# A state-space scan in front of a GELU feed-forward block, one core: VectorE's steps on w_out, the transfers, and the sums of w_in in another order around the first group

## The chip, the cores and the metric

The kernel runs on one core of a Trainium2 chip. A core has five engines that run side by side, each with its own queue that is worked off in order: TensorE (PE, matrix products), VectorE (DVE), ScalarE (ACT), GpSimd (POOL) and SyncE (SP, which here issues nearly all DMA transfers). The metric is the time of one execution on the device in microseconds (us), lower is better; a kernel's time is the median of its runs.

## What is computed

The reference has two blocks. The first is a state-space recurrence (Mamba-2 style) over 4 batches, 8 heads and 768 positions, in chunks; the second is a feed-forward block with an approximate GELU on the 3072 tokens of 256 features that the first one leaves:

```python
# per batch and head; cum is the running sum of log a in a chunk
L = exp(cum_i - cum_j) * causal
y_intra = ((C @ B.T) * L) @ x
y_inter = (C @ state) * exp(cum)
state = exp(sum of log a) * state + sum_j B_j x_j exp(cum_last - cum_j)
# on tokens x 256
h = x @ w_in                      # 256 x 2048
g = h * sigmoid(1.702 * h)
out = g @ w_out                   # 2048 x 256
```

`w_in` and `w_out` come as 64-bit floats. The chip computes in 32 bits, so the kernel reads them as 32-bit words and makes the 32-bit floats itself.

## The kernel before, in words

**Groups and pairs.** The 3072 tokens are six groups of 512. A group is two *pairs* (`PG` = 2), a pair two chunks of 128 tokens. So group 0 holds pairs 0 and 1, group 1 pairs 2 and 3, and so on. While TensorE does the feed-forward products of one group, the other engines prepare the recurrence of the next.

**Group 0** does its feed-forward block plainly: `hidden(0, f)` for f from 0 to 15 (line 893; two products by a block of 128 columns of `w_in`, and SiLU on ScalarE), then `project_all` (line 989), which goes through f = 0 to 15 again with the rows of `w_out`. From group 1 on, each block goes by seven products in place of eight (`first`, `product`, lines 933 and 1030); that needs sums of blocks of the weights (`mix_in` for w_in, line 907, `mix_w` for w_out) and of the data (`mix_y`, `mix_g`).

**The weights** come in ten pieces (`PIECES`, line 154): pieces 0 to 5 are `w_in`, 6 to 9 `w_out`, four blocks each for the large ones. One piece takes these steps:

- `fetch(i)` (line 163): two DMAs on SP into one of four buffers;
- `fields(i)` (lines 192, 195): two VectorE steps that cut out exponent and mantissa;
- `clamp(i)` (lines 203, 204): two ScalarE steps on the exponent;
- `rounded(i)` (line 208): one VectorE step on the mantissa;
- `join(i)` (lines 222, 228): VectorE, two steps for each part; the second writes `w_in` or `w_out`. Only now can TensorE use the piece.

`narrow(i)` (line 235) is the VectorE part of one turn: `rounded(i)`, `join(i)`, and `fields(i + 1)`, in an order that hangs on i. `project_all` needs piece 6 at f = 0, piece 7 at f = 4, 8 at f = 8 and 9 at f = 12.

**The recurrence of pairs 2 and 3.** A pair needs its decay matrix L, made by a VectorE scan over the a values. For pair 2 the values are fanned out by TensorE (`fan_all`, line 424) into PSUM, and four scans read them there (`decay_heads`, line 457); `ends` (line 468) makes the values at chunk ends (tile Be); `since_fanned` (lines 548, 550) makes the decay since a chunk's start for the last chunks of batch 0, out of another PSUM bank. For pair 3 the values go by way of DRAM: `store_a` clips them on VectorE (line 358) and writes them to `scratch` (line 1232), `spread(3)` (line 261) reads them back to all partitions (tile a), and `decay(3)` (line 409) scans. `spread_rows(1)` (line 270) reads the a values of batch 1 (tile af); `clip_rows(1)` and `decay_rows(1)` (lines 487 to 500; VectorE, then POOL, then VectorE) turn them into the decay since the chunk's start. `turn(p)` transposes B and C of a pair on TensorE (line 604), copies them on ScalarE (line 597), and ends with `since_start` (line 674, tile CsT) on VectorE, which for pairs 2 and 3 reads the transposed C in its PSUM bank. `gain` (line 720, tile A) multiplies B by x for the states and takes the PSUM banks that the transposes of the two pairs used. Then come `score` (line 689), the additions of `keep_both` (line 789), `weigh` (line 700), and `finish` (lines 829 and 843), which leaves the input of group 1's feed-forward block.

**What sets the order.** Everything is written out by hand: `at(in_hidden[0], f, ...)` puts work behind `hidden(0, f)`, `at(in_project[0], f, ...)` ahead of the products of f in `project_all`. Entries of one place run in the order in which the `at` calls were made. A last step ties every engine's queue to the order of the program, so a waiting instruction holds all that stands behind it on its engine. PSUM gives the feed-forward products four banks in turn; the fanned rows, transposes, `gain` and `project_all`'s two sums take their banks from the same four.

Of the kernel before, what the change touches and what calls it, by code (L numbers as in the profile page):

```python
# [16 lines left out]
P = 128  # L17
# [18 lines left out]
def kernel(  # L36
# [48 lines left out]
    PG = CG // 2  # L85
# [52 lines left out]
    def load(p, parts=None):  # L138
        if parts is None:
            parts = "bcx" if p < 2 * PG else "bx"  # L140
            if p >= 2 * PG:
                load_blocks(p)
        for part in parts:
            dst, src, e = {"b": (rb, B, N), "c": (rc, C, N), "x": (rx, x, D)}[part]
            dst[p] = raw.tile([P, 2, NH, e], FP32, tag=part, name=f"{part}{p}",
                              bufs=2 if part == "c" else 3)
            for k in range(2):
                b, c = divmod(2 * p + k, NC)
                sl = slice(c * P, (c + 1) * P)
                nc.sync.dma_start(out=dst[p][:, k], in_=src[b, :, sl, :].rearrange("h s d -> s h d"))  # L150
# [12 lines left out]
    def fetch(i, held=False):  # L163
        name, f, n = PIECES[i]
        if n == 2 and f % 4:
            t = pieces.pop(i - 1)[:, 2 * n * DM:]
        else:
            t = pieces[i] = words(f"bits{i}")
            t = t[:, :2 * n * DM]
        if held:  # L170
            held.memset(t[:, :1], 0)
        if name == "in":
            src = moe_w_in[:, 2 * f * P:2 * (f + n) * P].rearrange("(k p) e -> p k e", p=P)
            dst, src = (v.rearrange(s, h=n, e=2 * P) for v, s in (
                (t, "p (h k e) -> k p h e"), (src, "p k (h e) -> k p h e")))
        else:
            src = moe_w_out[f * P:(f + n) * P, :].rearrange("(f p) (h e) -> h p f e", p=P, h=2)
            dst = t.rearrange("p (h f e) -> h p f e", h=2, f=n)
        for k in range(2):
            nc.sync.dma_start(out=dst[k], in_=src[k])  # L180
        t = t.rearrange("p (e w) -> p e w", w=2)
        bits[i] = t[:, :, 0], t[:, :, 1]
# [5 lines left out]
    def fields(i):  # L188
        hi, cols = bits[i][1], slice(0, PIECES[i][2] * DM)
        mantissa[i] = wide.tile([P, PN], U32, tag="m", name=f"m{i}")[:, cols]  # L190
        power[i] = wide.tile([P, PN], U32, tag="p2", name=f"p2{i}")[:, cols]
        nc.vector.tensor_scalar(out=power[i], in0=hi, scalar1=0x7FF00000, scalar2=None,
                                op0=ALU.bitwise_and)

        nc.vector.tensor_scalar(out=mantissa[i], in0=hi, scalar1=0x000FFFFF,
                                scalar2=0x00100000, op0=ALU.bitwise_and, op1=ALU.bitwise_or)
# [18 lines left out]
    def join(i, parts=1):  # L215

        name, f, n = PIECES[i]
        n //= parts
        low, m, p2 = bits.pop(i)[1], mantissa.pop(i), power.pop(i)
        for k in range(parts):  # L220
            cols, fs = slice(k * n * DM, (k + 1) * n * DM), slice(f + k * n, f + (k + 1) * n)
            nc.vector.scalar_tensor_tensor(out=p2[:, cols], in0=low[:, cols], scalar=0x80000000,
                                           in1=p2[:, cols], op0=ALU.bitwise_and, op1=ALU.bitwise_or)
            if name == "in":
                dst, h = w_in[:, fs].rearrange("p f k e -> p (f k e)").unsqueeze(1), 1
            else:
                dst, h = w_out[:, :, fs].rearrange("p c f e -> p c (f e)"), 2
            nc.vector.scalar_tensor_tensor(  # L228
                out=dst, in0=m[:, cols].bitcast(FP32).rearrange("p (h e) -> p h e", h=h),
                scalar=2.0 ** -20, in1=p2[:, cols].bitcast(FP32).rearrange("p (h e) -> p h e", h=h),  # L230
                op0=ALU.mult, op1=ALU.mult)
        for n in NEXT.get(i, ()):
            fetch(n)

    def narrow(i):
        rounded(i)
        if i in (2, 4, 5):
            join(i, 1 if i == 2 else 2)
        if i == 4:
            clip(az[:, CG:], 1)  # L240
        if i + 1 < len(PIECES):
            fields(i + 1)
        if i not in (2, 4, 5):
            join(i, 2 if i == 3 else 1)


# [3 lines left out]
    def spread(p, held=False):  # L250

        if p - 2 in ra:
            ra[p] = ra[p - 2]
        else:
            ra[p] = words(f"a{p}").bitcast(FP32)[:, :2 * NH * H].rearrange(
                "p (k e) -> p k e", k=2)
        if held:
            nc.vector.memset(ra[p][:, 0, :1], 0.0)
        b, c = divmod(2 * p, NC)
        for i, side in enumerate(SIDES):  # L260
            nc.sync.dma_start(
                out=ra[p][side],
                in_=scratch[c:c + 2, i, b * NH:(b + 1) * NH].rearrange("c h i -> c (h i)").unsqueeze(
                    0).to_broadcast([H, 2, NH * H]))
# [3 lines left out]
    def spread_rows(b):  # L268
        raf[b] = raw.tile([P, NC, P], FP32, tag="af", name=f"af{b}", bufs=1)
        nc.sync.dma_start(out=raf[b].rearrange("p c s -> p (c s)"),  # L270
                          in_=a[b].unsqueeze(1).to_broadcast([NH, N, S]))
# [84 lines left out]
    def clip(t, name):  # L356

        nc.vector.tensor_scalar(out=t, in0=t, scalar1=1e-6, scalar2=1.0,
                                op0=ALU.max, op1=ALU.min)
        if name:  # L360
            starts[name] = const.tile([P, t.shape[1], 2], FP32, name=f"starts{name}")
        first = t.rearrange(by_chunk, s=2)[:, :, :, 0]
        if name:
            nc.vector.tensor_copy(starts[name], first)
        nc.vector.memset(first, 0.0)
# [58 lines left out]
    def fan_all(p):  # L424

        ab = area(f"ab{p}")[:, :, :2 * Q * H]
        for r in range(R):
            fan(p, r, ab[:, r])
        fan_since()
        for r in range(R):  # L430
            decay_heads(p, r, ab[:, r])
        for k in range(2):
            ends(p, k)
# [99 lines left out]
    def fan_since():  # L533
        o = bank("rows4")
        t = fanned["rows"] = fan_rows(az, CG, NC, o)
        f = fanned["starts"] = o[:, 2 * P:2 * P + 2 * (NC - CG)]
        nc.tensor.matmul(out=f, lhsT=whose[:32, 0].rearrange("p h n -> p (h n)"),
                         rhs=starts[1][:32].rearrange("p c s -> p (c s)"), start=True, stop=True,
                         tile_position=(0, 0), skip_group_check=True)
# [678 lines left out]
    join(1)  # L1218
    fields(2)
    clamp(2)  # L1220
    load(PG)


    def at(places, i, *work):
        places.setdefault(i, []).extend(work)
# [5 lines left out]
        for i, side in enumerate(SIDES):  # L1231
            nc.sync.dma_start(out=scratch[:, i].rearrange("c r i -> r c i"), in_=az[:32, :, side])

    at(in_hidden[0], 5, lambda: fetch(7), lambda: fetch(8), lambda: load(PG + 1))
    at(in_hidden[0], 7, lambda: pick_a(PG))
    at(in_hidden[0], 9, lambda: fan_all(PG))
    at(in_hidden[0], 9, since_fanned, store_a)
    for i, k, c in ((2, 1, 1), (3, 2, 2), (4, 4, 7), (5, 8, 11), (6, 11, 14), (7, 14, 15)):
        at(in_hidden[0], k, lambda i=i: narrow(i))
        at(in_hidden[0], c, lambda i=i: clamp(i + 1))  # L1240
    at(in_hidden[0], 9, lambda: spread(PG + 1), lambda: spread_rows(1))
    n, p = 2 * PG, 3 * PG
    pairs = PG, PG + 1
    at(in_project[0], 0, lambda: turn(PG), lambda: rounded(8),
       lambda: fields(9), lambda: join(8))
    at(in_project[0], 1, lambda: clamp(9))
    at(in_project[0], 2, lambda: decay(PG + 1), lambda: clip_rows(1),
       lambda: decay_rows(1), lambda: turn(PG + 1))
    at(in_project[0], 5, lambda: narrow(9))
    at(in_project[0], 9, lambda: score(pairs), lambda: gain(pairs), lambda: keep_both(pairs, True),  # L1250
       lambda: weigh(PG), lambda: weigh(PG + 1))
    at(in_project[0], 15, lambda: finish(pairs))
    at(in_project[0], 13, lambda: mix_in(1), lambda: spread(n + 1, held=True),
       lambda: load(n + 1, "x"), lambda: mix_in(2), lambda: mix_in(3),
       lambda: turn_blocks(2), lambda: decay(n))
    at(in_project[0], 6, lambda: spread(n), lambda: load(n), lambda: load_blocks(n + 1),
       lambda: load(n + 1, "b"))

# [4 lines left out]
    at(after, "H0", lambda: decay(n + 1), lambda: mix_y(1), lambda: since_start(n),  # L1263
       lambda: since_start(n + 1), lambda: gain(later), lambda: keep_both(later, True), lambda: score(later),
       lambda: weigh(n), lambda: weigh(n + 1))
    at(after, "H1", lambda: turn_out(0, 0), lambda: turn_out(0, 1))
    assert [b for b in range(NB) if 3 * CG <= b * NC < 4 * CG] == [2]


# [58 lines left out]
        z=lambda: finish(later, (0,)), y=lambda: finish(later, (1,)), W=lambda: mix_w(0))  # L1328
    for j in range(2):
        mix_g(1, j)  # L1330
    run(1, "4.1 4.5 4.2 P P 4.6 P L P 4.7 P P P 4.D", seven(1, 0), L=more_loads)
    mix_w(1)
    mix_g(1, 2)
    decay(p)
# [118 lines left out]
```

## Time and profile before

| what | value |
|---|---|
| median of 3 runs | 354.91 us (353.28 to 355.25) |
| the profiled execution | 355.53 us, its span 353.8 us |
| PE busy | 342.8 us, 97% of the span |
| DVE busy | 255.3 us, 72% |
| ACT busy | 155.2 us, 44% |
| POOL busy | 13.8 us, 4% |
| `hidden(0, f)` on PE, from f = 3 on | about 23.4 to 47.7 us |
| `project_all` on PE, with pair 2's and 3's work in it | 50.0 to 87.1 us |
| `hidden(1, f)`, then the seven-product blocks | from 87.1 us |

Times of the trace count from the start of the span. A line of a timeline has start, duration, engine, line and operation, output and inputs, the shape, and how many instructions were merged into it; in brackets is the idle time of the engine just before it and what ended it. A PE product of 128x512 shows a duration of about 0.6 us, but the next one starts 0.43 us after it. In `hidden` and `project_all` one f takes four such records. In the table of stretches, a row has the stretch, its length, then for PE, PEld (weight loads), DVE, ACT and POOL the busy time and the number of instructions, the granted clock of TensorE (1.00 is full), the DMA share and the rate in GB/s.

### The profile page before, as it was taken

What the parts mean: (1) busy time and instruction counts of PE and PEld (TensorE: products, weight loads), DVE (VectorE), ACT (ScalarE), POOL (GpSimd) and SP (SyncE); (2) the same over time, 40 slices, a digit from 0 to 9 for tenths busy, and PEclk for the clock granted to TensorE, in tenths of its full rate; (3) what the DMA queues carried; (4) which work ended last, traced back from release to release, by engine and by line L of the source; (5) the groups of instructions that cost most, each with busy time, mean ns of one, the idle gap of its engine ahead of it and who ended that gap; (6) DMA issues with size and microseconds to landing.
All of it is one profiled execution on the core that took longest, in us unless ns stands there. A gap on an engine that the chain in (4) does not pass through costs nothing.

```text
span 353.8 us, 8134 instructions
## 1 busy us (share of the span) xinstructions
PE 342.8 (97%) x3380; PEld 269.3 (76%) x3380; DVE 255.3 (72%) x485; ACT 155.2 (44%) x352; POOL 13.8 (4%) x42
## 2 busy tenths in 40 slices
PE   8899989699999999999999999999999999999996
PEld 6534434345588888888888888888888888889996
DVE  4889997699857999687799387689375555465463
ACT  5788765013653241655333455333455331453320
POOL 7400000100000000000000000000000000000000
PEclk9999999989999999999999999999999999999999
DMA  5699896654542500226724006510000210000401
GB/s 147 144 314 189 202 178 167 126 85 96 104 76 85 109 0 2 48 44 127 130 30 76 0 16 124 101 19 3 0 4 3 40 21 0 0 2 0 61 1 59
DMA packets 89980, 25.92 MB, mean 73 GB/s; under 512 B 73432, under 2 KB 87128, under 8 KB 89944
## 3 DMA queue, kind: packets, MB, share of 16 engines
q1 hardware_dynamic: 89112, 24.88, 34.0%
q10 hardware_dynamic: 832, 0.52, 0.5%
q8 instruction: 26, 0.43, 0.5%
q14 instruction: 10, 0.08, 0.1%
HBM read 22.15 MB, written 3.24 MB: 72 GB/s over the span
## 4 chain that ended last, share of the span: by engine, by line
PE 73%; DVE 9%; DMA 8%; SPq 4%; issue 2%; ACT 2%; POOL 1%; ACTq 0%; DVEq 0%; POOLq 0%
PE acc L1059 25%; PE X L954 17%; PE Y L964 13%; PE acc L1066 7%; PE o L996 4%; DMA af<-in_a_dram 3%; DMA az<-in_a_dram 2%; SPq L180 2%; PE h L899 2%; PE y L843 2%; DMA a<-scratch 2%; PE cb L689 1%; PE y L829 1%; DMA bits<-in_moe_w_in_dram 1%; PE A L720 1%
## 5 line engine op out<-in xcount | busy, mean ns | idle before, releaser
L959 ACT ACTIVATE ac<-X 128x256 f32<-128x256 f32 x76 | 29.1, 382 | 81.5 <-PE X L954 80.7
L1086 DVE TENSOR_TENSOR gT<-Y,ac 128x512 f32<-128x512 f32 x38 | 26.2, 689 | 41.4 <-PE Y L964 32.2
L1059 PE MATMUL acc<-mg,mw 128*128 128x256 f32 x192 | 54.5, 379 | 0.0
L931 ACT ACTIVATE gT<-gT 128x512 f32<-128x512 f32 (+1 forms) x76 | 38.9, 519 | 30.4 <-DVE gT L1086 29.9
L954 PE MATMUL X<-my,mi 128*128 128x256 f32 x152 | 45.2, 380 | 0.3 <-ACT ac L959 0.3
L1059 PEld LDWEIGHTS acc<-mg,mw 128*128 128x128 f32 x192 | 36.5, 190 | 5.0
L1086 DVE TENSOR_TENSOR gT<-Y,b 128x256 f32<-128x256 f32 x38 | 15.8, 419 | 28.5 <-PE Y L964 28.5
L899 PE MATMUL h<-yT,w_in 128*128 128x512 f32 x80 | 35.6, 597 | 0.5 <-ACT yT L862 0.5
L1059 PE MATMUL acc<-gT,w_out 128*128 128x256 f32 x128 | 35.6, 380 | 0.0
L954 PEld LDWEIGHTS X<-my,mi 128*128 128x128 f32 x152 | 28.0, 190 | 4.4 <-ACT ac L959 0.7
L996 PE MATMUL o<-gT,w_out 128*128 128x512 f32 x64 | 29.4, 614 | 1.7 <-DVE w_out L228 1.7
L899 PEld LDWEIGHTS h<-yT,w_in 128*128 128x128 f32 x80 | 14.8, 190 | 18.9 <-issue 15.5
L922 DVE TENSOR_TENSOR mg<-gT 128x512 f32<-128x512 f32 x40 | 27.2, 681 | 0.0
L1059 PEld LDWEIGHTS acc<-gT,w_out 128*128 128x128 f32 x128 | 24.2, 190 | 3.6 <-ACT yT L877 0.3
L996 PEld LDWEIGHTS o<-gT,w_out 128*128 128x128 f32 x64 | 12.3, 197 | 16.1 <-issue 14.1
L959 ACT ACTIVATE b<-X 128x256 f32<-128x256 f32 x38 | 14.6, 383 | 20.7 <-PE X L954 20.2
L954 PE MATMUL X<-yT,w_in 128*128 128x256 f32 x76 | 23.2, 389 | 0.0
L964 PE MATMUL Y<-yT,w_in 128*128 128x256 f32 x76 | 22.7, 381 | 0.0
L964 PE MATMUL Y<-my,mi 128*128 128x256 f32 x76 | 22.7, 380 | 0.0
L964 PE MATMUL Y<-yT,mi 128*128 128x256 f32 x76 | 22.6, 381 | 0.0
L409 DVE TENSOR_TENSOR_SCAN L<-a,idents 128x1024 f32<-128x1024 f32 x9 | 20.5, 2280 | 2.9 <-DMA a<-scratch 2.9
L954 PE MATMUL X<-my,w_in 128*128 128x256 f32 x76 | 22.5, 379 | 0.0
(159 smaller groups left out, 547.2 us busy)
## 6 DMA issues: line engine op xcount, KB each, us to landing
a<-scratch SPq DMA_DIRECT2D x18, 256.0 KB, 4.8
bits<-in_moe_w_out_dram SPq DMA_DIRECT2D x8, 512.0 KB, 6.2
x<-in_x_dram SPq DMA_DIRECT2D x24, 128.0 KB, 3.5
out_dram<-ob SPq DMA_DIRECT2D x40, 64.0 KB, 2.0
bits<-in_moe_w_in_dram SPq DMA_DIRECT2D x8, 256.0 KB, 4.4
bits<-in_moe_w_in_dram SPq DMA_DIRECT2D x4, 512.0 KB, 12.1
b<-in_B_dram SPq DMA_DIRECT2D x20, 64.0 KB, 3.5
af<-in_a_dram SPq DMA_DIRECT2D x3, 384.0 KB
```

What stands on the lines that cost most here:

```text
L180: nc.sync.dma_start(out=dst[k], in_=src[k])
L409: nc.vector.tensor_tensor_scan(out=L, data0=ra[p].rearrange("p k e -> p (k e)"), data1=idents.rearrange("p h i -> p (h i)"), initial=0.0, ...
L899: nc.tensor.matmul(out=h, lhsT=w_in[:, f, k], rhs=yT[g][:, k], start=(k == 0), stop=(k == NK - 1), skip_group_check=True)
L922: nc.vector.tensor_tensor(out=t[:, 0:2], in0=B[:, :, 1], in1=B[:, 0], op=ALU.subtract)
L931: nc.scalar.activation(o, i, AF.Silu, scale=GELU_SCALE)
L954: nc.tensor.matmul(out=s["X"], lhsT=lhsT, rhs=rhs, start=i == "1", stop=i == "4", skip_group_check=True)
L959: nc.scalar.activation(copy, s["X"], AF.Copy)
L964: nc.tensor.matmul(out=o, lhsT=lhsT, rhs=rhs, start=s.pop("new", False), stop=i != "5", skip_group_check=True)
L996: nc.tensor.matmul(out=o[c], lhsT=w_out[:, c, f], rhs=gT[g, f // 2][:, f % 2], start=(f == 0), stop=(f == NF - 1), skip_group_check=True)
L1059: nc.tensor.matmul(out=acc[g][0][i][:, cols], lhsT=w, rhs=h[:, cols], start=(j == 0 and k == 0 and (i, 0) in begins), stop=(j == NF // 2 - ...
L1066: nc.tensor.matmul(out=o[k] if type(o) is list else o[:, cols], lhsT=h[:, cols], rhs=w, start=(j == 0 and (i, k) in begins), stop=(j == NF ...
L1086: nc.vector.tensor_tensor(out=o, in0=v, in1=w, op=ALU.add)
```

## The change

`narrow(6)` joins piece 6 ahead of `fields(7)`, with `since_fanned` in between; `clamp(6)` and `narrow(6)` stand behind `hidden(0, 10)`, not 11. `fan_all` only fans; the scans and `ends` of pair 2 stand in a new `decay_fanned` behind `hidden(0, 15)`. `store_a` and its two writes to `scratch` move from f = 9 to f = 5, ahead of the fetches of pieces 7 and 8. The x transfers of pairs 2 and 3 move behind `spread_rows(1)` and `spread(3)`, and these two change places. In `project_all`, `join(8)` goes ahead of `fields(9)`, `clip_rows(1)` ahead of `decay(3)`, `turn(3)` moves from f = 2 to f = 4, and `score`, `gain`, `keep_both` and `weigh` of pairs 2 and 3 from f = 9 to f = 10. Of the sums of w_in, `mix_in(2)` and `mix_in(3)` leave f = 13: one goes behind `hidden(1, 3)`, the other ahead of the steps on block 4 of group 1, where `more_loads` also stands now. Nothing is computed more or less than before.

```diff
     def narrow(i):
         rounded(i)
-        if i in (2, 4, 5):
-            join(i, 1 if i == 2 else 2)
+        if i in (2, 4, 5, 6):
+            join(i, 2 if i in (4, 5) else 1)
         if i == 4:
             clip(az[:, CG:], 1)
+        if i == 6:
+            since_fanned()
         if i + 1 < len(PIECES):
             fields(i + 1)
-        if i not in (2, 4, 5):
+        if i not in (2, 4, 5, 6):
             join(i, 2 if i == 3 else 1)
...
         fan_since()
+        fans[p] = ab
+
+    def decay_fanned(p):
+
+        ab = fans.pop(p)
         for r in range(R):
             decay_heads(p, r, ab[:, r])
         for k in range(2):
...
-    load(PG)
+    load(PG, "bc")
...
-    at(in_hidden[0], 5, lambda: fetch(7), lambda: fetch(8), lambda: load(PG + 1))
+    at(in_hidden[0], 5, store_a, lambda: fetch(7), lambda: fetch(8),
+       lambda: load(PG + 1, "bc"))
     at(in_hidden[0], 7, lambda: pick_a(PG))
     at(in_hidden[0], 9, lambda: fan_all(PG))
-    at(in_hidden[0], 9, since_fanned, store_a)
-    for i, k, c in ((2, 1, 1), (3, 2, 2), (4, 4, 7), (5, 8, 11), (6, 11, 14), (7, 14, 15)):
+    for i, k, c in ((2, 1, 1), (3, 2, 2), (4, 4, 7), (5, 8, 10), (6, 10, 14), (7, 14, 15)):
         at(in_hidden[0], k, lambda i=i: narrow(i))
         at(in_hidden[0], c, lambda i=i: clamp(i + 1))
-    at(in_hidden[0], 9, lambda: spread(PG + 1), lambda: spread_rows(1))
+    at(in_hidden[0], 15, lambda: decay_fanned(PG))
+    at(in_hidden[0], 9, lambda: spread_rows(1), lambda: spread(PG + 1),
+       lambda: load(PG, "x"), lambda: load(PG + 1, "x"))
     n, p = 2 * PG, 3 * PG
     pairs = PG, PG + 1
     at(in_project[0], 0, lambda: turn(PG), lambda: rounded(8),
-       lambda: fields(9), lambda: join(8))
+       lambda: join(8), lambda: fields(9))
     at(in_project[0], 1, lambda: clamp(9))
-    at(in_project[0], 2, lambda: decay(PG + 1), lambda: clip_rows(1),
-       lambda: decay_rows(1), lambda: turn(PG + 1))
+    at(in_project[0], 2, lambda: clip_rows(1), lambda: decay(PG + 1),
+       lambda: decay_rows(1))
+    at(in_project[0], 4, lambda: turn(PG + 1))
     at(in_project[0], 5, lambda: narrow(9))
-    at(in_project[0], 9, lambda: score(pairs), lambda: gain(pairs), lambda: keep_both(pairs, True),
+    at(in_project[0], 10, lambda: score(pairs), lambda: gain(pairs), lambda: keep_both(pairs, True),
        lambda: weigh(PG), lambda: weigh(PG + 1))
     at(in_project[0], 15, lambda: finish(pairs))
     at(in_project[0], 13, lambda: mix_in(1), lambda: spread(n + 1, held=True),
-       lambda: load(n + 1, "x"), lambda: mix_in(2), lambda: mix_in(3),
-       lambda: turn_blocks(2), lambda: decay(n))
+       lambda: load(n + 1, "x"), lambda: turn_blocks(2), lambda: decay(n))
...
-    at(after, "H1", lambda: turn_out(0, 0), lambda: turn_out(0, 1))
+    at(after, "H1", lambda: turn_out(0, 0), lambda: turn_out(0, 1), lambda: mix_in(2))
...
-    run(1, "4.1 4.5 4.2 P P 4.6 P L P 4.7 P P P 4.D", seven(1, 0), L=more_loads)
+    more_loads()
+    mix_in(3)
+    run(1, "4.1 4.5 4.2 P P 4.6 P P 4.7 P P P 4.D", seven(1, 0))
```

## The prediction

> **What bounds the kernel now.** The page's first part says that PE is busy for 97% of the span, so I ask where PE waits. The view of who waited for whom, for PE alone from 20 to 130 us, has three rows (us in total, times, longest):
>
> ```profile
> PE A L720 <- DVE CsT L674: 2.9, 1, 2.9
> PE o L996 <- DVE w_out L228: 1.7, 1, 1.7
> PE X L954 <- ACT ac L959: 0.3, 1, 0.3
> ```
>
> The first two lie in the stretch that the change rewrites. The table of stretches, cut at them, shows what else they cost:
>
> ```profile
> 48.30:50.04 1.74, 0.04 (x2) 0.03 (x1) 1.71 (x3) 1.44 (x2) 0.00 (x0) 1.00 0.73 73
> 50.04:67.53 17.49, 17.49 (x106) 8.21 (x106) 13.02 (x15) 6.59 (x10) 0.00 (x0) 1.00 0.77 168
> 67.53:70.38 2.85, 0.00 (x0) 0.00 (x0) 2.24 (x3) 0.00 (x0) 0.87 (x3) 0.94 0.31 65
> 70.38:73.87 3.49, 3.49 (x58) 2.04 (x59) 3.46 (x4) 1.69 (x8) 0.19 (x1) 0.56 0.88 120
> 73.87:85.37 11.50, 11.50 (x207) 6.04 (x205) 11.18 (x24) 0.00 (x0) 0.00 (x0) 1.00 0.37 78
> ```
>
> The reader is to see that PE does nothing for 1.7 us ahead of `project_all` and for 2.85 us in it, and that right after the second wait the granted clock is 0.56 for 3.49 us. After the first it stays at 1.00. PE's timeline prices this:
>
> ```profile
> 53.98 12.18 PE L996 MATMUL o<-gT,w_out 128*128 128x512 f32 x28
> 66.09 1.21 PE L689 MATMUL cb<-CT,BT 32*64 32x128 f32 x64
> 67.23 0.30 PE L720 MATMUL A<-x,Be 64*32 64x64 f32 x2
> 70.38 1.10 PE L720 MATMUL A<-x,Be 64*32 64x64 f32 x54 [2.85 <-DVE CsT L674]
> 71.41 11.57 PE L996 MATMUL o<-gT,w_out 128*128 128x512 f32 x24
> 82.91 1.04 PE L829 MATMUL y<-CsT,S 32*64 32x64 f32 x56
> ```
>
> 28 records take 66.09 - 53.98 = 12.11 us, 0.4325 each; the 24 after the wait take 82.91 - 71.41 = 11.50 where 10.38 were due: 1.12 lost. The A products take 0.30 + 1.03, and 0.83 for the same 56 later (90.64 to 91.47): 0.50 lost. **All in all 1.71 + 2.85 + 1.12 + 0.50 = 6.2 us** can be won here. From 23.4 to 130 us PE otherwise stands back to back, but for the 0.3 us of the third row.
>
> Why the waits? The timeline of DVE:
>
> ```profile
> 39.76 0.69 DVE L192 TENSOR_SCALAR p<-bits 128x1024 uint32<-128x1024 uint32 x1
> 40.97 2.43 DVE L457 TENSOR_TENSOR_SCAN L<-ab,idents 128x256 f32<-128x256 f32 x4
> ...
> 47.41 1.22 DVE L222 SCALAR_TENSOR_TENSOR p<-bits,p 128x1024 uint32<-128x1024 uint32 x1
> 48.67 1.22 DVE L228 SCALAR_TENSOR_TENSOR w_out<-m,p 128x1024 f32<-128x1024 f32 x1
> ...
> 62.36 2.29 DVE L409 TENSOR_TENSOR_SCAN L<-a,idents 128x1024 f32<-128x1024 f32 x1 [2.17 <-DMA a<-scratch]
> 66.90 0.56 DVE L487 TENSOR_SCALAR af<-af 128x768 f32<-128x768 f32 x1 [1.73 <-DMA af<-in_a_dram]
> 68.01 1.76 DVE L500 TENSOR_TENSOR_SCAN since<-af,first 128x768 f32<-128x768 f32 x1 [0.55 <-POOL af L493]
> 69.90 0.42 DVE L674 TENSOR_TENSOR CsT<-tp,since 128x256 f32<-128x256 f32 x1
> ```
>
> DVE is full up to 60 us, and piece 6 stands behind pair 2's decay, the store and `fields(7)`; then DVE waits three times, 2.17 + 1.73 + 0.55 us, for transfers and POOL. The chain of waits goes the same way (SP's issues from 13 to 24 us, the az transfer to 32.9, DVE, the af transfer from 57.56 to 66.88, DVE, A). SP issued a<-scratch only at 56.16, after the scratch writes (51.15 and 51.64) had landed.
>
> **The change, part by part.** I follow each queue with durations from start to next start.
>
> *DVE to 55.* The clip of `store_a`, 0.44 (44.64 to 45.08), now comes after `fields(5)` ends at 35.16. It falls into the 0.68 us that DVE waited for ACT ahead of 37.10: nothing. `fields(6)` ends at 40.97 as before. Then `rounded(6)` 1.13 to 42.1. `join(6)` needs `clamp(6)`: ACT is free at 40.0 and the exponents are there at 40.45, so it runs to 40.45 + 2.3 = 42.8; the SiLU of f = 11 waits behind it to 43.3, and PE has other banks until then. `join(6)` takes 2.40 (47.41 to 49.81) and ends at **45.2; PE needs it at 48.3**. `since_fanned` 0.80 to 46.0, `fields(7)` 1.20 to 47.2, `rounded(7)` 1.14 to 48.4, `fields(8)` 1.20 to 49.6, `join(7)` 2.40 to 52.0; due at f = 4, 48.3 + 6.9 + 0.4 for the second transposes = 55.6. The moved decay and `ends` take 2.87 (40.97 to 43.84): to 54.9.
>
> *DVE from 55.* CsT of pair 2, 0.34, `rounded(8)` 1.13, `join(8)` 2.40: 58.8, due at f = 8, 62.6. `fields(9)` to 60.0, clip of af 0.6 to 60.6, decay and ends of pair 3, 2.75, to 63.4 (POOL's 0.55 lies beside it), scan 1.85 and CsT 0.34: **65.6**. PE starts at 48.3, takes 40 records (17.3) and the transposes (0.43), is at f = 10 at 66.0, does cb in 1.14, and wants the A bank at **67.2**. `narrow(9)` 3.54 to 69.1, due at f = 12: 68.0 + 3.5 = 71.5. ACT's copies of A end at 69.8, the additions (1.76) at 71.6, `weigh` (2.26) at 73.8, due for `finish` at f = 15: 68.0 + 8.65 = 76.6. So both waits go, with 1.6 to 3.8 us to spare.
>
> *SP and the DMA queues.* All this stands only if af and a have landed by 60.0 and 60.6, and x of both pairs by 67.2. SP's issues go on without a hole from 29 to 51: b and c of pair 2 to 36.0, now scratch (0.93; its data are ready at 35.6), pieces 7 and 8 (3.0) to 40.0, b and c of pair 3 (7.2) to 47.2, piece 9 (1.7) to 48.9, af to 49.6, a to 51.0, x to 53.9. Piece 8 issues 0.7 earlier than before. Landing: before, a and af (issued 56.16 to 58.28) landed at 62.3 and 66.9 with two more a in between. Piece 9, issued 0.5 earlier and without x ahead of it, lands near 53.5; 896 KB of af and a at 133 GB/s (1408 KB of a, af, a from 58.0 to 68.6) take 6.7 more: af near 56.5, a near 60.2. The bounds for a are 57 (issue at 51.0 and the 6.1 of before) and 63; x behind it, 56 to 66 (by the 9.6 us that the a transfers issued at 59.04 took behind af: 63.5). 63 for a would make CsT 2.4 later and PE wait 0.8. I take none, since 60.2 is the nearer row.
>
> *The bank of the fanned rows* is held to 46.0, before to 44.7. PE's products ran back to back from 37.33 to 47.7 although it was held, so the other three banks fed them. If f = 13 got this one, PE would wait from 42.5 to 46.0; I take zero, bounds 0 and 3.5.
>
> *After `finish`.* f = 15, then two blocks of group 1 (3.52): PE wants A of pairs 4 and 5 at 84.4, before at 90.64. DVE: `mix_in(1)` 1.45 to 75.3. The two others, 2.9, no longer stand ahead, but `turn_blocks` needs the B and C blocks, landed at 78.4 before, behind a queue of SP that hardly moves: the same number of transfers must land first (zB waited 3.3 us for af's landing). With s as what that queue gains: transposes end at 79.5 - s, decay of pair 4 at 82.3 - s; a of pair 5 was held by a one-column memset on DVE (line 258) at 79.3, SP was ready at 78.1, so it lands at 83.5 - s instead of 84.8; Be of pair 5 is ready at 86.3 - s, needed at 84.4 + 0.4. **A new wait of 1.5 - s, between 0 and 1.5**; SP's hole of 4 us ahead of 56.16 goes, but the queue behind is held by landings, so I take s = 0.8, 0.7 us. The first wait, of 1.7, cost no clock, so neither should this one.
>
> *`mix_in(2)` and `mix_in(3)`.* 1.45 each. The first falls into the 3.05 us that DVE was idle ahead of 101.06, the second into the 1.74 ahead of 109.97. `more_loads` has its memset at the same place of DVE's queue. Nothing; if the second cover were gone, 1.45 at most.
>
> **The sum:** -6.2 + 0.7 = -5.5. The profiled execution took 355.53 (span 353.8, 1.7 around it), 0.6 above the median of the runs. 355.53 - 5.5 = 350.0; against the median, 354.91 - 5.5 = **349.4**, which I predict.
>
> **The rivals.**
> - *The slow clock stays*, because something else brought it. For: the wait's own row has 0.94, so the slow stretch began about when PE resumed, not within the wait. Against: it follows PE's longest wait, and the table has no other row below 0.94. Then 1.6 stays: 351.0. The Trainium skill (TensorE: Matmul & The Clock Gate, Part 1) has the clock halve after an idle window of some 3.4 us; by that rule a wait of 2.85 us should not do it, which speaks for this rival, while the trace shows 0.56 behind just such a wait.
> - *Transfers late, gain halved.* a at 63 to 65 or the rows' bank costs 1 to 3.5 us: 350.4 to 353.
> - *No measurable change*: the upper bounds together (0.8 for a, 3.5 for the bank, 1.5 in place of 0.7 for Be) take 5.1 of the 5.5: 354.5.
> - *Slower: x of pairs 2 and 3 lands after its need.* x is the one thing that the change puts later in SP's queue, behind 896 KB of slow broadcasts. From 67.2 on each us is a us of PE; beyond 2.85 the clock's 1.6 comes back. Landing at 71.1 eats all of the gain (5.5 = 3.9 + 1.6), 72.9 makes it slower by over 0.5%. For: transfers behind af and a took 9.6 us. Against: that from 53.9 gives 63.5. 357 or more.
>
> **How the numbers follow.** A measurement of this kernel can tell about 0.5% (1.8 us) from no change. Forecast 0.70 (348.7 to 350.2, by the bounds of the new wait), clock stays 0.07, gain halved 0.08: faster 0.85. Within 0.5%: 0.08. Slower: 0.07. The range takes in the first three: from all 6.2 us and half a us of scatter, 348.2, to 352.8.
>
> **What would show it.** Right: w_out L228 for piece 6 ends near 45.2 and o starts at 48.3; no wait of A on CsT, and 1.00 in the clock column from 48 to 96; A of pairs 4 and 5 near 85. Wrong: A waiting on x or on CsT, h waiting on `since`, a wait on Be above 1.5 us, or a DVE row of `mix_in` ahead of a waiting PE after 90.

## The result, and the profile after

The changed kernel takes 350.2 us (348.73 to 350.7, 6 runs), the kernel before 354.4 beside it (353.12 to 357.69, 6 runs): a ratio of 0.9865, 95% interval 0.9818 to 0.9913, or 4.8 us of 354.4. (This is the ratio of the means, 349.91 and 354.69; the medians differ by 4.2 us.) The forecast was 349.4, 5.5 us less than before. The profiled executions differ by 355.53 - 350.48 = 5.05 us, their spans by 353.8 - 348.5 = 5.3. PE comes to group 1's first product by blocks at 91.28 in place of 96.13.

Who PE waited for from 20 to 130 us, in the changed kernel (us in total, times, longest):

```profile
PE A L727 <- DVE Be L475: 1.3, 1, 1.3
PE X L961 <- ACT ac L966: 0.2, 1, 0.2
```

Both rows that the forecast wanted gone are gone, and the wait that it named for the other end is there. (Lines moved by 2 to 7: L727 is the former L720, L475 the former L468, L1003 the former L996.) The table of stretches, cut at `project_all`, at cb and A of pairs 2 and 3, and at the new wait:

```profile
48.24:65.94 17.70, 17.70 (x46) 7.80 (x45) 17.43 (x23) 7.95 (x12) 2.46 (x3) 1.00 0.81 166
65.94:67.80 1.86, 1.86 (x122) 1.60 (x121) 1.86 (x3) 0.00 (x0) 0.47 (x1) 1.00 0.72 171
67.80:84.88 17.08, 17.08 (x253) 8.54 (x248) 13.18 (x21) 6.38 (x18) 0.00 (x0) 1.00 0.58 98
84.88:86.16 1.28, 0.00 (x1) 0.00 (x0) 1.25 (x3) 0.23 (x1) 0.00 (x0) 1.00 0.23 65
```

PE is busy for all of the first three, at a granted clock of 1.00; before, the same work had holes of 1.74 and 2.85 us and 3.49 us at 0.56. The fourth row is the new hole. DVE's timeline shows the three due dates that went from late to early, and what holds up the fourth:

```profile
44.10 1.22 DVE L228 SCALAR_TENSOR_TENSOR w_out<-m,p 128x1024 f32<-128x1024 f32 x1
...
61.13 2.28 DVE L411 TENSOR_TENSOR_SCAN L<-a,idents 128x1024 f32<-128x1024 f32 x1
...
65.74 0.42 DVE L681 TENSOR_TENSOR CsT<-tp,since 128x256 f32<-128x256 f32 x1
...
83.49 2.29 DVE L411 TENSOR_TENSOR_SCAN L<-a,idents 128x1024 f32<-128x1024 f32 x1 [2.80 <-DMA a<-scratch]
```

Piece 6 is joined by 45.3 (wanted at 48.2), pair 3's decay starts without a wait in brackets, CsT is there at 66.2 (wanted at 67.1). The decay of pair 5 waits 2.80 us for its a values, and PE waits for its Be.

### The profile page after: what moved, and what is told of

It is laid out like the page before. It is cut to its first block, busy times and chain, and to the rows that moved or that the text cites. A ratio compares the mean times of both kernels' runs of the same rounds, so it can differ in the third digit from the quotient of the medians.

```text
span 348.5 us, 8128 instructions
## 1 busy us (share of the span) xinstructions
PE 341.5 (98%) x3380; PEld 269.2 (77%) x3380; DVE 255.5 (73%) x485; ACT 155.0 (44%) x352; POOL 15.3 (4%) x42
## 4 chain that ended last, share of the span: by engine, by line
PE 72%; DVE 9%; SPq 7%; DMA 5%; issue 3%; ACT 3%; POOL 0%; DVEq 0%; POOLq 0%; ACTq 0%
PE acc L1066 25%; PE X L961 17%; PE Y L971 13%; PE acc L1073 7%; DMA a<-scratch 5%; SPq L150 4%; PE y L850 2%; PE cb L696 2%; DVE p L222 2%; DVE L L411 1%; PE y L836 1%; SPq L124 1%; ACT p L204 1%; PE A L727 1%; PE h L906 1%
## 5 line engine op out<-in xcount | busy, mean ns | idle before, releaser
L961 PE MATMUL X<-my,mi 128*128 128x256 f32 x152 | 45.2, 380 | 0.2 <-ACT ac L966 0.2
L1003 PE MATMUL o<-gT,w_out 128*128 128x512 f32 x64 | 28.3, 595 | 0.0
L1003 PEld LDWEIGHTS o<-gT,w_out 128*128 128x128 f32 x64 | 11.8, 190 | 13.6 <-issue 13.2
```

Source lines behind the costliest of these rows:

```text
L961: nc.tensor.matmul(out=s["X"], lhsT=lhsT, rhs=rhs, start=i == "1", stop=i == "4", skip_group_check=True)
L1003: nc.tensor.matmul(out=o[c], lhsT=w_out[:, c, f], rhs=gT[g, f // 2][:, f % 2], start=(f == 0), stop=(f == NF - 1), skip_group_check=True)
```

## The experiments

All runs, with the kernel before run on the same chip. The last column has PE's waits of 0.16 us and more between 40 and 90 us, in the one profiled execution of each.

| run | median, before beside it, us | ratio, 95% interval | PE waits on |
|---|---|---|---|
| e1_dve_only | 355.03, 354.15 | 1.0030, 1.0004 to 1.0057 | CsT 3.87 |
| e2_transfers_only | 350.44, 354.15 | 0.9902, 0.9873 to 0.9932 | ahead of o 1.20 |
| e3_sums_back | 349.76, 354.15 | 0.9889, 0.9854 to 0.9924 | Be 0.52 |
| e4_a_before_b | 348.65, 354.15 | 0.9846, 0.9817 to 0.9875 | none |
| e4_again | 348.81, 354.21 | 0.9849, 0.9808 to 0.9890 | none |
| e5_x_early | 351.17, 355.44 | 0.9889, 0.9839 to 0.9938 | none (see there) |
| e5_again | 350.03, 354.21 | 0.9877, 0.9826 to 0.9927 | CsT 0.52 |
| e6_store_late | 348.91, 355.44 | 0.9820, 0.9776 to 0.9863 | Be 0.72 |
| after_again | 349.61, 355.44 | 0.9849, 0.9800 to 0.9899 | none |
| e7_af_first_only | 350.69, 353.41 | 0.9902, 0.9865 to 0.9940 | CsT 0.38, Be 0.58 |
| e8_a_first | 349.54, 353.41 | 0.9874, 0.9834 to 0.9913 | Be 0.16 |

The theory: the new order of the transfers of pair 3's a values and of af ends the long wait, VectorE's order on w_out ends the short one, and the short one is worth nothing as long as the long one stands. The first two runs take the change apart along that line. Neither has the moves within `project_all` (`clip_rows(1)` ahead of `decay(3)`, `turn(3)` at f = 4, the products of the pairs at f = 10); no run tries these by themselves.

**VectorE's order alone, on the kernel before.**

```diff
 # narrow, fan_all, decay_fanned as in the change; then
-    at(in_hidden[0], 9, since_fanned, store_a)
+    at(in_hidden[0], 9, store_a)
-    ... (5, 8, 11), (6, 11, 14), ...
+    ... (5, 8, 10), (6, 10, 14), ...
+    at(in_hidden[0], 15, lambda: decay_fanned(PG))
-       lambda: fields(9), lambda: join(8))
+       lambda: join(8), lambda: fields(9))
```

> The kernel before with VectorE's new order on w_out alone (piece 6 joined ahead of fields(7), pair 2's decay behind hidden(0, 15), join(8) ahead of fields(9)); transfers, store and sums stay. Theory (the af transfer ends the second wait, whatever PE does ahead of it): o starts at 48.3 in place of 50.0, but CsT still comes near 69.9, so the 1.7 us come back as a longer wait of A, about 4.6 us in place of 2.9, and the half clock stays: 354.4 us, ratio 0.998 to 1.002. Rival (two independent waits, each worth its own length): 352.7 us, ratio 0.995. Rival (the order on VectorE is what brings the gain): 350.2 us.

Measured: 1.0030 (1.0004 to 1.0057), no gain, if anything a loss of 1 us. PE's wait and the clock, in stretches of its span, with the kernel before under it in stretches of its own:

```profile
66.00:67.50 1.50, 0.00 (x0) 0.00 (x0) 0.95 (x2) 0.00 (x0) 0.32 (x2) 1.00 0.52 107
67.50:69.10 1.60, 0.00 (x0) 0.00 (x0) 1.47 (x3) 0.00 (x0) 0.53 (x1) 0.51 0.15 41
69.10:74.40 5.30, 5.28 (x59) 2.71 (x60) 5.04 (x10) 1.69 (x8) 0.20 (x1) 0.50 0.64 89
74.40:82.70 8.30, 8.30 (x20) 3.42 (x18) 8.20 (x17) 0.00 (x0) 0.00 (x0) 1.00 0.48 97
```

```profile
66.60:67.50 0.90, 0.90 (x50) 0.59 (x34) 0.56 (x1) 0.00 (x0) 0.00 (x0) 1.00 0.51 141
67.50:70.00 2.50, 0.03 (x1) 0.00 (x0) 1.86 (x2) 0.00 (x0) 0.49 (x3) 1.00 0.29 69
70.00:73.40 3.40, 3.02 (x57) 1.81 (x58) 3.37 (x4) 1.69 (x8) 0.57 (x1) 0.51 0.87 111
```

The wait ahead of o is gone and the one of A has grown from 2.85 to 3.87 us, with CsT at 68.64: PE only came earlier to the same gate. It grew by less than the 1.7 expected; CsT itself came 1.26 us earlier (before at 69.90), as the a transfers were issued at 54.93, 1.2 us before those of the kernel before. And the longer wait costs more clock: half rate from 67.5 to 74.4, 6.9 us, where before it had 3.4. The 24 records after it take 82.73 - 70.16 = 12.57 us, 2.19 over the 10.38 due, in place of 1.12. The other executions point the same way: the mean granted clock was 0.995 or less in 11 of the 12 of this kernel, and in 5 of the 17 of the kernel before beside it. So the two waits are not independent, and both rivals fall.

**The transfers alone, on the kernel before.**

```diff
-    load(PG)
+    load(PG, "bc")
-    at(in_hidden[0], 5, lambda: fetch(7), lambda: fetch(8), lambda: load(PG + 1))
+    at(in_hidden[0], 5, store_a, lambda: fetch(7), lambda: fetch(8),
+       lambda: load(PG + 1, "bc"))
-    at(in_hidden[0], 9, since_fanned, store_a)
+    at(in_hidden[0], 9, since_fanned)
-    at(in_hidden[0], 9, lambda: spread(PG + 1), lambda: spread_rows(1))
+    at(in_hidden[0], 9, lambda: spread_rows(1), lambda: spread(PG + 1),
+       lambda: load(PG, "x"), lambda: load(PG + 1, "x"))
```

> The kernel before with the new order of the transfers alone (store_a at f = 5, spread_rows(1) ahead of spread(3), x of pairs 2 and 3 behind them); VectorE's order on w_out and the sums stay. Theory: a lands near 61, CsT comes near 67 and A waits 0 to 0.4 us, so the 2.85 us and the slow clock's 1.6 go; the wait on piece 6 stays but for the 0.44 us of the clip, 1.3 us; Be of pair 5 comes near 86.7 and makes PE wait 0.5: 350.0 us (349.5 to 351), nearly all of the change. Rival (the transfers help only where VectorE is early too): 353 us or more. Rival (the clock stays slow whatever the wait): 351.6 us.

Measured: 0.9902 (0.9873 to 0.9932), 3.5 us of 354.15. Of PE's waits only the first is left; the row names ACT, whose SiLU ended at 49.3, 0.1 us behind the join of piece 6:

```profile
PE o L996 <- ACT gT L902: 1.2, 1, 1.2
PE X L954 <- ACT ac L959: 0.4, 1, 0.4
```

The wait on CsT and the slow clock go without anything done for w_out, and without the moves within `project_all`. The wait on Be that I expected, 0.5 us, did not come: Be of pair 5 was ready at 85.3, wanted at 85.5. With VectorE's order on top, the changed kernel has 0.9865 and 0.9849 in its two measurements; the intervals overlap, so that the 1.2 us more are seen in the trace, not in the times.

**The sums of w_in back at f = 13, in the changed kernel.**

```diff
-       lambda: load(n + 1, "x"), lambda: turn_blocks(2), lambda: decay(n))
+       lambda: load(n + 1, "x"), lambda: mix_in(2), lambda: mix_in(3),
+       lambda: turn_blocks(2), lambda: decay(n))
# and mix_in(2), mix_in(3), more_loads out of their new places
```

> The changed kernel with mix_in(2) and mix_in(3) back at f = 13, and more_loads at its old place. Theory (Be of pair 5 is held by the landing of its a values, and the 2.9 us of sums fall into VectorE's 2.8 us of idle time ahead of it): PE waits about 1.3 to 1.6 us on Be as in the changed kernel, 350.2 us, ratio to the changed kernel 0.999 to 1.002. Rival (the sums stand on the path ahead of A of pairs 4 and 5): wait 2.5 to 4.2 us, 351.5 to 353 us, more if the clock halves.

Measured: 0.9889 (0.9854 to 0.9924), the wait on Be 0.52 us: the move of the sums is worth nothing that these runs can show. The 2.9 us of sums fill the time in which VectorE otherwise waits for a of pair 5; its scan starts right behind the step ahead of it, with no wait in brackets:

```profile
82.44 2.28 DVE L411 TENSOR_TENSOR_SCAN L<-a,idents 128x1024 f32<-128x1024 f32 x1
```

That the wait is shorter than the changed kernel's 1.28 is no merit of the sums: a landed by 82.4 in this execution and at 83.4 in that one.

**The a values of pair 5 ahead of its b values, in the changed kernel.**

```diff
-       lambda: load(n + 1, "x"), lambda: turn_blocks(2), lambda: decay(n))
+       lambda: load(n + 1, "bx"), lambda: turn_blocks(2), lambda: decay(n))
-    ... lambda: load_blocks(n + 1),
-       lambda: load(n + 1, "b"))
+    ... lambda: load_blocks(n + 1))
```

> The changed kernel with the b transfers of pair 5 behind its a transfers instead of ahead of them. Theory (a of pair 5 lands 6 us after SP issues it, and the two b issues hold it up by 1.1 us): a lands near 82.4, decay of pair 5 starts 1.1 us earlier, PE waits 0.2 to 0.5 us on Be or x in place of 1.3: 349.2 to 349.6 us where the changed kernel has 350.2. Rival (what sets the landing is how much the DMA engines have left in all): no change, 350.2 us, wait 1.0 us or more.

> The changed kernel with the b transfers of pair 5 behind its a transfers, once more, on another chip: PE waits less than 0.3 us on Be, ratio to the kernel before 0.981 to 0.986, a little under that of the changed kernel (0.985 to 0.9865).

Measured: 0.9846 (0.9817 to 0.9875) and 0.9849 (0.9808 to 0.9890). In the issues of SP the b transfers no longer stand ahead; first the changed kernel, then this one:

```profile
75.59 1.01 SPq L150 DMA_DIRECT2D b<-in_B_dram  x2
76.71 1.24 SPq L263 DMA_DIRECT2D a<-scratch  x2
78.54 1.28 SPq L150 DMA_DIRECT2D x<-in_x_dram  x2
```

```profile
75.15 1.24 SPq L263 DMA_DIRECT2D a<-scratch  x2
76.48 1.16 SPq L150 DMA_DIRECT2D b<-in_B_dram  x2
78.33 2.69 SPq L150 DMA_DIRECT2D x<-in_x_dram  x2
```

And the decay of pair 5, in this kernel's DVE timeline:

```profile
80.99 2.29 DVE L411 TENSOR_TENSOR_SCAN L<-a,idents 128x1024 f32<-128x1024 f32 x1 [1.31 <-PE o L1003]
```

It starts 2.5 us earlier, and what ends DVE's idle time is no longer the transfer but PE, which comes out of `project_all`. The view of PE's waits has no row left between 20 and 130 us, in both profiles. The spans are 346.7 and 346.8 us against 348.5 and 347.3 of the changed kernel (e8 below has 346.8 too). By time the difference, 0 to 0.7 us by the ratios, does not stand clear of the changed kernel's interval.

**What of the transfers it is.** The remaining runs undo the moves of the transfers in the changed kernel, one at a time, and in e7 two of them.

```diff
# e5: x early again
+    load(PG)  ...  lambda: load(PG + 1)
# e6: the store late again
+    at(in_hidden[0], 9, store_a, lambda: spread_rows(1), lambda: spread(PG + 1), ... x)
# e7: both
+    load(PG)  ...  lambda: load(PG + 1)
+    at(in_hidden[0], 9, store_a, lambda: spread_rows(1), lambda: spread(PG + 1))
# e8: a ahead of af again
+    at(in_hidden[0], 9, lambda: spread(PG + 1), lambda: spread_rows(1), ... x)
```

> The changed kernel with the x transfers of pairs 2 and 3 back at their old places, ahead of the fetches of pieces 7 and 8 and of af and a. Theory (x ahead of a puts a back by some 2 us, since x of pair 3 stands in the same queue, and VectorE needs a at 61): a lands at 62 to 63, CsT comes at 67.5 to 68.5, A waits 0.3 to 1.5 us on it, too short for the clock: 350.3 to 351.7 us where the changed kernel has 350.2. Rival (it is x that has to be late for a gain at all): a lands as before the change, the wait is 2.5 us or more, 353 us or more. Rival (x is hidden wherever it stands): 350.2 us and no wait.

The first profile of it can't tell: PE stood still for 2.0 us in the first group, with nothing in the profile that it waited for, the clock halved, and all that PE does behind it came 4.4 us later (o at 52.61), so that every transfer was early for it. The rows of that start:

```profile
15.00:18.40 3.40, 1.40 (x84) 1.11 (x78) 3.30 (x8) 1.66 (x3) 0.00 (x0) 1.00 1.02 315
18.40:25.20 6.80, 6.33 (x63) 3.43 (x62) 3.87 (x9) 4.68 (x9) 0.00 (x0) 0.50 1.08 339
```

> The changed kernel with the x transfers early, once more, since the first profile of it has a half clock at 18 to 25 us that sets the whole first group back by 4 us and hides what the place of x does. Theory: with no half clock at the start, a lands 1 to 2 us later than in the changed kernel, A waits 0.3 to 1.5 us on CsT; 350 to 351.5 us. Rival (the holes of the DMA engines near 35 us take x of pair 2, and x of pair 3 costs SP and the engines less than 1 us): no wait of A on CsT, 349.5 to 350.3 us.

Measured: 0.9877, a wait of 0.52 us on CsT; a kept VectorE waiting to 62.78. The theory's lower end: x early costs half a microsecond in the trace, which the times can't tell from nothing.

> The changed kernel with store_a back at f = 9, ahead of spread_rows(1) and spread(3). Theory (a is held by what the DMA engines have to move ahead of it, piece 9 and af, and not by SP's issue): the scratch writes land near 51, a is issued near 52 in place of 48.4 and still lands at 60 to 62: 350.2 to 351 us, wait of A on CsT 0 to 1 us. Rival (the early store is what lets a come early): a lands 3.5 us later than in the changed kernel, near 64.5; A waits 3 us and the clock halves: 353 us or more.

Measured: 0.9820 (0.9776 to 0.9863), no wait on CsT. a was issued at 52.95, 4.5 us later than in the changed kernel, and landed by 58.8, earlier than there (60.9). The early store is not needed, as long as af is issued ahead of a. (The ratio is the lowest of all, but the changed kernel measured beside it, the next run, has 0.9849, and the intervals overlap.)

> The changed kernel as it is, beside the two others on the same chip: 350.2 us, ratio 0.985 to 0.989 to the kernel before; the wait of A on Be of pair 5 is the one that moves from one execution to another, with the landing of its a values, 0.5 to 1.5 us.

Measured: 0.9849, and the view of PE's waits has no row between 20 and 130 us: a of pair 5 landed by 82.4, 1 us earlier than in the first profile.

> The changed kernel with two of the three moves of the transfers undone: store_a at f = 9 again and x of pairs 2 and 3 early again; only af ahead of a is left, with VectorE's new order. Theory (of the old order it is the hole that counts, in which SP waits for the scratch writes before it issues a and, behind it, af): af is issued near 51 beside the scratch writes, a near 56 and lands at 62 to 63; VectorE clips af while it waits; CsT comes at 67.3 to 68, A waits 0.3 to 1 us: 350 to 351 us, ratio 0.986 to 0.990. Rival (the early store and the late x are both needed): a lands at 65 or later, A waits 3 us or more, the clock halves: 353 us or more.

Measured: 0.9902 (0.9865 to 0.9940); a is issued at 56.74, waits 0.38 us on CsT and 0.58 on Be. With nothing but af issued (at 51.54) while the scratch writes are under way, most of the gain stays: 3.5 us of 353.41, where the changed kernel has 4.8 and 5.4 in its two measurements. Its DVE timeline shows why:

```profile
60.55 0.55 DVE L494 TENSOR_SCALAR af<-af 128x768 f32<-128x768 f32 x1
62.52 2.29 DVE L411 TENSOR_TENSOR_SCAN L<-a,idents 128x1024 f32<-128x1024 f32 x1 [1.41 <-DMA a<-scratch]
```

The a values are no earlier than in the kernel before (62.36 there); but af, which was the last to land at 66.88, is there by 60.55, and its clip and POOL's part lie ahead of the scan and beside it.

> The changed kernel with spread(3) ahead of spread_rows(1) again; store_a early and x late stay. Theory (both transfers are issued 8 us earlier than before, so that their order no longer matters): a lands near 58, af near 61; VectorE waits 0 to 1 us for af, CsT comes at 65.7 to 66.7, before the 67.1 at which PE needs its bank: no wait on CsT, ratio 0.983 to 0.987 as the changed kernel. Rival (af behind a is late as before, 4.6 us behind it): CsT at 68 or later, A waits 1 us or more, 351 us or more.

Measured: 0.9874 (0.9834 to 0.9913), no wait on CsT, which came at 65.3. With the store early, either order of a and af will do. So the moves of the transfers insure each other: af must not stand behind a transfer that waits for the scratch writes, and either the early store or the other order sees to it.

## Why the prediction was right

- *What bounds.* Right: the two waits and the slow clock were 6.2 us of PE in the profiled execution, and in e4's profile all of it is won: from the transposes ahead of `project_all` to group 1's first product by blocks PE takes 89.67 - 47.68 = 41.99 us, before 96.13 - 47.73 = 48.40. PE's path from o's first product to group 1's first product by blocks is 91.28 - 48.24 = 43.04 in the changed kernel and 96.13 - 50.04 = 46.09 before; the difference of 3.05 and the 1.71 ahead of it make 4.8, which is 6.2 less the new wait, 1.28, to 0.2.
- *What the sum was of: the term of the slow clock was too large for most executions.* The 1.12 + 0.50 = 1.6 us of slow clock come from one execution, with a mean granted clock of 0.995 (3.4 us at half rate in 354 us make just that), and the forecast took them off a median. Of the 50 executions of the kernel before that ran beside the experiments, 20 had 0.995 or less, at a mean of 355.8 us, and 30 had 0.999 or 1.000, at 353.5; the changed kernel had 0.995 in one of 12. So most executions had no such term to win. That fits a measured gain which is 0.7 us (by means) to 1.3 us (by medians) short of 5.5; where the low clock lay in executions without a profile is not on record.
- *The walk along VectorE.* Right to 0.8 us: `join(6)` 45.2 forecast and 45.3 measured, `join(7)` 52.0 and 52.8, `join(8)` 58.8 and 59.5, CsT 65.6 and 66.2, A wanted at 67.2 and started at 67.08.
- *a lands near 60.2, bounds 57 and 63.* 60.9 in the changed kernel, 59.0 in its second profile. Right, but not for SP: I had it done with x at 53.9, and it stood in the four x issues from 49.76 to 61.26. x still landed in time (the third of the four at 63.56; A began without a wait at 67.08). The rival of x coming too late did not occur in any profile.
- *The new wait: mis-sized too.* The prediction took 0.7, between 0 and 1.5; the first profile has 1.28, the kernel's second none, the other runs 0 to 0.72. That 0.7 lies between is luck, for the reason given was another: I had a of pair 5 take as long to land as before. It was issued 2.7 us earlier (76.71, before 79.37) but took 6.0 us in place of 4.8. SP's issues before the change:

```profile
77.07 1.01 SPq L150 DMA_DIRECT2D b<-in_B_dram  x2
79.37 1.24 SPq L261 DMA_DIRECT2D a<-scratch  x2
84.77 1.01 SPq L150 DMA_DIRECT2D x<-in_x_dram  x2
```

  Two things are new: b goes ahead by 1.1 us in place of 2.3, and x of pair 5, which before waited for PE's y until 84.77, is now issued at 78.54, while a is under way. e4 shows that moving b is enough: with b behind a, and x at nearly the same time (78.33), the wait is gone. Whether x takes anything from a is open; no run holds x back by itself.
- *The slow clock* went with the wait (1.00 throughout, 40 to 90 us), so the rival of its staying falls, and e1 shows the other direction: a longer wait, a longer slow stretch. The Trainium skill (TensorE: Matmul & The Clock Gate, Part 1) says that the window that decides runs freely and lasts some 3.4 us. The trace agrees on both: 3.4 us at half rate before and 6.9 in e1 are one and two such windows, and the changes of clock stand on one grid (see the last section). It does not agree that PE must be idle for all of one: 2.85 us were enough.
- *The sums and the rows' bank* cost nothing, as taken: PE stood back to back from 37.40 on through the fanned rows' longer hold (to 46.1).

## What to carry to other kernels

Of two waits one behind the other on the same engine, closing the first alone gains little as long as what ends the later one stays where it is: here it gained nothing (e1), and closing the second alone brought most (e2). Before reordering an engine's steps, look at which transfer is the last to land, and whether it stands in its queue behind one that must wait for something else. An earlier finish also uncovers the next wait: the one on Be of pair 5 took back up to 1.3 of 6.2 us, until a was issued ahead of b (e4). And a cost read in one profile is the cost of one execution: the slow clock stood in that profile, but the granted clocks of the other runs show none in 30 of 50.

## What the runs showed of the hardware

- In the one profiled execution of each kernel, a wait of 1.7 us cost no clock, one of 2.85 us cost 3.4 us at half rate, one of 3.87 us cost 6.9 us. The clock fell at 70.05 and rose at 73.46 before the change, at 67.54 and 74.36 in e1, and at 18.37 and 25.19 in e5's first profile; the trace's record of the full rate begins at 5.20, 6.10 and 4.71. Every stretch between two of these times is a whole number of windows of 3.41 us, so that they stand on one grid. In the window just ahead of each fall PE was busy for 0.89, 1.12 and 1.41 us. In windows of such a grid that hold a shorter wait it was busy for 2.17 us (the wait on piece 6 before the change), 2.21 (the same wait in e2) and 2.65 (the new wait), and the clock stayed. So in these traces the fall goes with little work in a window, and not with the length of one wait alone. Where between 1.41 and 2.17 us the border lies, and whether the small products of cb and A count in full, no run shows. By this the same wait can cost clock in one execution and none in the next, depending on where it falls on the grid, which would fit the 20 and 30 executions above; that is argued, not shown.
- One cause of the scatter of the runs, some 4 us, can lie at the very start: in e5's first profile PE stood still for 2.0 us amid y of group 0, with nothing in the profile that it waited for (0.9 in the changed kernel), the clock was half from 18.4 to 25.2, and o began 4.4 us late. The span was 2.8 us longer than the changed kernel's, which has the wait of 1.28 us on Be that this one lacks.
- An issue can hold SP for long: the four x issues behind af and a took 11.5 us of SP in the changed kernel (49.76 to 61.26), 9.3 in e2 and 4.6 in e6, where a was issued later; before the change, with neither ahead of them, two took 1.6 (36.01 to 37.63). That the rows of a and af, which go to all partitions, are what held them was not tried by itself.
